# Opening of a fused attention and FFN kernel: the norm weight multiplied earlier, one tile's transposes copied by two engines, and a quarter of a later k load moved forward

## The chip, the cores and the metric

The kernel runs on one core of one Trainium2 chip. The metric is the device time of one execution in microseconds (us), lower is better. Before the change it took 326.73 us (median of 3 runs, 326.69 to 327.09). Engines: PE does matmuls and transposes, PEld loads its weights, DVE is VectorE, ACT is ScalarE, POOL is GpSimd, SP issues most DMAs.

## The reference, cut to what matters

```python
def _attn_ref(q, k, v):                      # q, k, v: (8, 8, 576, 64), float32
    # phi(x) = concat(relu(x) * cos, relu(x) * sin), angle grows with the position
    kv  = einsum('bhsf,bhsd->bhfd', phi(k), v);  z = sum(phi(k), axis=2)
    return einsum('bhsf,bhfd->bhsd', phi(q), kv) / (einsum('bhsf,bhf->bhs', phi(q), z)[..., None] + 1e-6)

def _moe_ref(x, w_gate, w_val, w_out, rms_g):  # x: (4608, 512), d_ff 1536
    xn = x / sqrt(mean(x * x, -1) + 1e-6) * rms_g
    g = xn @ w_gate
    return (g * sigmoid(g) * (xn @ w_val)) @ w_out
```

The argument concerns the first 128 rows of x ("tile 0"). They must pass attention, the norm and a transpose before the first FFN matmul can start. Almost everything before that matmul is a chain of small, dependent steps; everything behind it is dense PE work.

## The kernel before: the parts that matter

```python
    load_kv("k", 0, *LOW); load_kv("k", 0, *HIGH); load_q_tokens(0, 0, 2)
    ...                                       # v of batch 0
    load_q_tokens(0, 2, 4)                    # last load of the opening on SP
...
def x_sq(b, j):        # ACT: sum of squares; POOL: rs = ms ** -0.5 (128x1)
    nc.scalar.activation(out=scr, in_=xt[:, 0 : DM + 1], func=AF.Square, scale=..., accum_out=ms)
    nc.gpsimd.tensor_tensor(out=rs, in0=ms, in1=mhalf, op=ALU.pow)

def x_norm(b, j):      # DVE: xn = (x * rs) * g in one pass, fp32 to bf16
    nc.vector.scalar_tensor_tensor(out=xn, in0=x_of[(b, j)][:, 0:DM], scalar=rs, in1=gb,
                                   op0=ALU.mult, op1=ALU.mult)
...
    kvz_mm(0, high_banks, (2, 3))
    nd_half(0, 0, 0, psV[0]);  nd_post_half(0, 0, 0, psV[0])    # tile 0, heads 0 to 3
    q_tr_evac(A, 0, 1, psO[0][:, :], (0, 4))
    ...
    nd_half(0, 0, 1, psO[1]);  nd_post_half(0, 0, 1, psO[1])    # tile 0, heads 4 to 7
    q_tr_evac(A, 0, 1, psO[0][:, :], (4, 8));  q_phi(A, 0, 2, 1)
    x_sq(0, 0)
    nd_pe(0, 1, psA);  nd_post(0, 1, psA)                       # tile 1
    q_phi(A, 0, 2, 0);  x_sq(0, 1)
    ...
    q_tr_pe(0, 2, psO[0][:, :])               # transposes of q, tile 2
    x_norm(0, 0)
    q_tr_evac(A, 0, 2, psO[0][:, :])          # ACT copies them out of PSUM
    q_phi(A, 0, 3, 1)                         # ACT: half of the q feature map of tile 3
    filler(1, psV[1][:, :])                   # a PE matmul on nothing
    ...
    x_tr_pe(0, 0, psG[1][:, :])               # four 128x128 transposes of xn
    x_tr_evac(V, 0, 0, psG[1][:, :])          # one DVE copy
    x_norm(0, 1);  q_phi(V, 0, 3, 0)
    open_ffn(0, (0, 1), 0, 128)               # the first FFN matmuls
    x_tr_pe(0, 1, psV[1][:, :]);  x_tr_evac(V, 0, 1, psV[1][:, :])
    nd_pe(0, 2, psA);  nd_post(0, 2, psA)     # needs q tile 2
    q_tr_pe(0, 3, psO[1][:, :])               # needs both halves of the map of q tile 3
```

In the timelines below each engine runs its instructions in the order of the program.

## Time and profile before

| | before |
|---|---|
| time, median of 3 | 326.73 us |
| span of the profile | 325.0 us |
| PE busy | 97% of the span |
| share of PE in the chain that ended last | 91% |
| first matmul of k times v | 10.86 us |
| first FFN matmul | 17.66 us |
| first matmul of the third gate slice | 22.35 us |

From the page of before: busy time by engine, and the chain by engine.

```profile
PE 316.5 (97%) x2410; PEld 161.8 (50%) x2445; DVE 185.8 (57%) x412; ACT 176.7 (54%) x366; POOL 31.9 (10%) x67
...
PE 91%; DMA 2%; ACT 2%; DVE 2%; issue 1%; SPq 1%
```

The kernel is bound by PE. So a change to other engines pays only where PE has holes. From the chain of waits of before, 10 to 24 us, in order of time; columns are start, length, who:

```profile
...
14.53 0.72 ACT scr L375 x2
15.25 0.62 ACT qp L209
15.88 0.05 issue
15.92 0.62 PE psO L254 x8
16.54 0.21 PE psV L466
16.76 0.40 PE psG L412 x4
17.16 0.02 issue
17.18 0.43 DVE xnT L265
17.62 0.04 issue
17.66 0.38 PE psG L566 x4
```

L466 is the filler, L412 the transposes of xn and L566 the FFN. From 17.66 us on PE goes gap-free for tens of us (the first wait is one of 0.30 us at 52.4). PE waited for the DVE copy only from 17.16 to 17.66 us, and for xn a little before that (the filler hides it). That is the ground the change wants to win.

The timeline of PE in before; columns are start, length, instruction, count, and in brackets the idle time before it:

```profile
10.86 0.20 PE L282 MATMUL psG<-vvm,kpm 64*128 64x65 bf16 x1
...
17.66 0.38 PE L566 MATMUL psG<-xnT,wg 128*128 128x128 bf16 x4 [0.52 <-DVE xnT L265]
...
18.77 0.41 PE L310 MATMUL psA<-kvzs,qpT 128*128 128x65 bf16 x8
19.02 0.61 PE L254 MATMUL psO<-ident,qp 128*128 128x128 bf16 x8
...
22.35 1.04 PE L566 MATMUL psO<-xnT,wg 128*128 128x256 bf16 x8
```

These lines serve as a ruler. "Third gate slice" stands for the first matmul with the third slice of w_gate (columns 512 to 767), into bank psO. It starts 22.35 - 10.86 = 11.49 us after the first k-times-v matmul, and the first FFN matmul 6.80 us after it. Note also that the transposes of q tile 3 (L254) follow the eight attention matmuls (L310) at 0.25 us, start to start: PE did not wait there.

### The profile page before, as it was taken

Reading aid. Unit: us, or ns where it says so; the run is one execution under the profiler, and the core shown is the slowest. Engines: PE = TensorE matmul, PEld = TensorE weight load, DVE = VectorE, ACT = ScalarE, POOL = GpSimd, SP = SyncE. Lnnn points to the kernel's source line nnn. Section 1 sums busy time; section 2 is a strip of 40 time slices with the busy share of each in tenths; the row PEclk is TensorE's granted clock in tenths of the full one; section 3 lists DMA queues with packets and bytes.
Section 4 is the critical chain, followed back from the end, with each engine's and each line's share of the span. In section 5 each row is a group of like instructions: output and inputs, shape, how many; then the busy total and the mean of one; then the engine's idle time right before and its main releaser. Section 6 shows DMA issues by size and latency. Waiting matters only on the chain.

```text
span 325.0 us, 6411 instructions
## 1 busy us (share of the span) xinstructions
PE 316.5 (97%) x2410; PEld 161.8 (50%) x2445; DVE 185.8 (57%) x412; ACT 176.7 (54%) x366; POOL 31.9 (10%) x67
## 2 busy tenths in 40 slices
PE   8899999999999999999999999999999999999995
PEld 2588465554445444554454445444544444444443
DVE  6875768787766765578257745773577134203410
ACT  6963865965674567545664475556644233223321
POOL 1660112001100110010001100110011000000000
PEclk9999999999999999999999999999999999999999
DMA  7999999998699666976597569957621400020014
GB/s 258 235 189 268 326 185 314 323 185 194 158 257 262 177 163 192 215 195 187 158 217 211 164 188 221 192 157 218 123 43 32 131 32 0 20 111 0 1 34 97
DMA packets 80305, 53.91 MB, mean 166 GB/s; under 512 B 51345, under 2 KB 67729, under 8 KB 80274
## 3 DMA queue, kind: packets, MB, share of 16 engines
q1 hardware_dynamic: 73232, 48.64, 57.7%
q0 software_dynamic: 6880, 4.72, 10.0%
q8 instruction: 19, 0.31, 0.4%
q10 hardware_dynamic: 162, 0.13, 0.2%
q14 instruction: 12, 0.10, 0.1%
HBM read 37.75 MB, written 9.44 MB: 145 GB/s over the span
## 4 chain that ended last, share of the span: by engine, by line
PE 91%; DMA 2%; ACT 2%; DVE 2%; issue 1%; SPq 1%
PE psC L446 26%; PE psG L426 26%; PE psV L426 26%; PE psA L282 3%; DMA rv<-in_v_dram 2%; PE psA L310 2%; PE psG L446 2%; PE psG L566 1%; PE psV L566 1%; PE psO L566 1%; ACT kpm L209 1%; PE psV L254 1%; ACT sg L435 0%; SPq L79 0%; PE psA L317 0%
## 5 line engine op out<-in xcount | busy, mean ns | idle before, releaser
L441 DVE TENSOR_TENSOR hT<-psV,sg 128x512 bf16<-128x512 f32 x102 | 70.3, 689 | 93.9 <-PE psV L426 69.1
L435 ACT ACTIVATE sg<-psG 128x512 f32<-128x512 f32 x102 | 60.6, 594 | 64.9 <-PE psG L426 63.4
L426 PE MATMUL psV<-xnT,wv 128*128 128x512 bf16 (+1 forms) x365 | 92.1, 374 | 0.4
L426 PE MATMUL psG<-xnT,wg 128*128 128x512 bf16 (+1 forms) x352 | 90.9, 374 | 0.7
L446 PE MATMUL psC<-wo,hT 128*128 128x512 bf16 x382 | 88.2, 379 | 0.7
L426 PEld LDWEIGHTS <-wv 128*128 128x128 bf16 x416 | 40.7, 98 | 47.4
L446 PEld LDWEIGHTS <-hT 128*128 128x128 bf16 x420 | 40.3, 98 | 46.6
L426 PEld LDWEIGHTS <-wg 128*128 128x128 bf16 x416 | 38.5, 98 | 41.0 <-DVE xnT L265 0.4
L263 ACT COPY osb<-psC 128x512 f32<-128x512 f32 (+1 forms) x33 | 19.1, 578 | 39.6 <-PE psC L446 38.9
L380 POOL TENSOR_TENSOR rs<-ms,mhalf 128x1 f32<-128x1 f32 x36 | 19.8, 549 | 199.4 <-ACT scr L375 199.4
L387 DVE SCALAR_TENSOR_TENSOR xn<-xt,rs,gb 128x512 bf16<-128x512 f32 x36 | 26.8, 746 | 17.1 <-POOL rs L380 17.1
L375 ACT ACTIVATE scr<-xt 128x513 bf16<-128x513 f32 x36 | 22.9, 635 | 22.8 <-DVE xt L364 22.7
L209 ACT ACTIVATE kpm<-rk,tab 128x256 bf16<-128x256 f32 (+1 forms) x78 | 31.9, 477 | 1.7 <-DMA rk<-in_k_dram 1.7
L364 DVE TENSOR_TENSOR xt<-psA,rec 128x512 f32<-128x512 f32 x35 | 24.2, 691 | 1.2
L211 DVE TENSOR_SCALAR kpm<-rk,tab 128x256 bf16<-128x256 f32 (+1 forms) x84 | 22.2, 330 | 2.2 <-DMA rk<-in_k_dram 2.2
L209 ACT ACTIVATE qp<-rq,tab 128x512 bf16<-128x512 f32 x32 | 22.4, 713 | 0.0
L211 DVE TENSOR_SCALAR qp<-rq,tab 128x512 bf16<-128x512 f32 x32 | 15.2, 488 | 0.0
L310 PEld LDWEIGHTS <-qpT 128*128 128x128 bf16 x248 | 11.6, 98 | 6.7 <-issue 0.3
L310 PE MATMUL psA<-kvzs,qpT 128*128 128x65 bf16 x248 | 12.8, 193 | 0.3
L426 PE MATMUL psG<-xnt_tail,wg 128*128 128x512 bf16 x48 | 12.3, 379 | 0.1
L426 PE MATMUL psV<-xnt_tail,wv 128*128 128x512 bf16 x47 | 12.1, 379 | 0.0
L282 PEld LDWEIGHTS <-kpm 64*128 64x128 bf16 x576 | 9.9, 94 | 3.7 <-issue 2.9
(89 smaller groups left out, 169.1 us busy)
## 6 DMA issues: line engine op xcount, KB each, us to landing
out_dram<-osb SPq DMA_DIRECT2D x32, 256.0 KB, 2.7
rk<-in_k_dram SPq DMA_DIRECT2D x20, 288.0 KB, 4.4
rq<-in_q_dram SPq DMA_DIRECT2D x20, 256.0 KB, 3.1
rv<-in_v_dram SPq DMA_DIRECT2D x17, 288.0 KB, 3.2
rv<-in_v_dram SPq DMA_DIRECT2D x5, 576.0 KB, 7.8
rk<-in_k_dram SPq DMA_DIRECT2D x2, 1152.0 KB, 8.4
rq<-in_q_dram SPq DMA_DIRECT2D x2, 1024.0 KB, 8.7
wo<-in_moe_w_out_dram POOLq DMA_DIRECT2D x4, 384.0 KB, 7.1
```

The costliest lines, as they stand in the source:

```text
L209: nc.scalar.activation(out=out_ap, in_=in_ap, func=AF.Relu, scale=scale)
L211: eng.tensor_scalar(out=out_ap, in0=in_ap, scalar1=scale, scalar2=0.0, op0=ALU.mult, op1=ALU.max)
L282: nc.tensor.matmul(banks[c][:, r * E : (r + 1) * E], lhsT=kp_main[b][lo : lo + 64, j, r, :], rhs=vvm[b % 2][lo : lo + 64, r, j, :], start= ...
L310: nc.tensor.matmul(o[:, g, i, :], lhsT=qpT[(b, 0)][:, h, j * P : (j + 1) * P], rhs=kvz_of(b, h), start=True, stop=True,)
L364: nc.vector.tensor_tensor(out=xt[:, 0:DM].rearrange("p (b h d) -> p b h d", b=2, d=D), in0=o[:, :, :, 0:D], in1=rec[:, :, :].unsqueeze(3). ...
L375: nc.scalar.activation(out=scr[:, :], in_=xt[:, 0 : DM + 1], func=AF.Square, scale=1.0 / math.sqrt(DM), accum_out=ms[:, :],)
L380: nc.gpsimd.tensor_tensor(out=rs[:, :], in0=ms[:, :], in1=mhalf[:, :], op=ALU.pow)
L387: nc.vector.scalar_tensor_tensor(out=xn[:, :], in0=x_of[(b, j)][:, 0:DM], scalar=rs_of[(b, j)][:, :], in1=gb[:, :], op0=ALU.mult, op1=ALU. ...
L426: nc.tensor.matmul(pst[bank][:, cols[0] : cols[1]], lhsT=w[:, t, n * P : (n + 1) * P], rhs=x[:, t, cols[0] : cols[1]], start=(t == 0), sto ...
L435: nc.scalar.activation(out=sg[:, :], in_=psG[bank][:, :], func=AF.Silu)
L441: nc.vector.tensor_tensor(out=hTs[blk][:, n, :], in0=psV[bank][:, :], in1=sg[:, :], op=ALU.mult)
L446: nc.tensor.matmul(bank, lhsT=hTs[blk][:, n, j * P : (j + 1) * P], rhs=wo[:, n, :], start=(n == 0), stop=(n == NNT - 1),)
```

## The change

The intent: take half of the norm's arithmetic off the path behind the mean square (x times g runs while ACT squares), drop the filler, copy the transposes with two engines, and use a hole of the DMA queue for a quarter of the next batch's k. The diff, cut to its core:

```diff
     load_q_tokens(0, 2, 4)
+    load_kv("k", 1, 0, 1)
@@
+    def x_gain(b, j, g):                       # DVE, 128x256: xg = x * gb, half g
+        c = slice(g * DM // 2, (g + 1) * DM // 2)
+        nc.vector.tensor_tensor(out=xg[:, c], in0=x_of[(b, j)][:, c], in1=gb[:, c], op=ALU.mult)
+    def x_scale(b, j):                         # DVE, 128x512: xn = xg * rs
+        nc.vector.tensor_scalar(out=xn[:, :], in0=xg[:, :], scalar1=rs_of[(b, j)][:, :], ...)
@@
     nd_post_half(0, 0, 0, psV[0])
+    x_gain(0, 0, 0)
@@
     nd_post(0, 1, psA)
+    x_gain(0, 0, 1)
@@
-    x_norm(0, 0)
-    q_tr_evac(A, 0, 2, psO[0][:, :])
-    q_phi(A, 0, 3, 1)
-    filler(1, psV[1][:, :])
+    x_scale(0, 0)
@@
-    x_tr_pe(0, 0, psG[1][:, :])
-    x_tr_evac(V, 0, 0, psG[1][:, :])
+    for half, (eng, bank) in enumerate(((A, psG[1]), (V, psV[1]))):
+        part = (2 * half, 2 * half + 2)
+        x_tr_pe(0, 0, bank[:, :], part)
+        x_tr_evac(eng, 0, 0, bank[:, :], part)
+    q_tr_evac(A, 0, 2, psO[0][:, :])
+    q_phi(A, 0, 3, 1)
@@
-    d = load_kv("k", 1)
+    d = load_kv("k", 1, 1, 4)
```

More of the change, by code (lines that the diff above doesn't have):

```diff
@@ L383 @@
     xn_of = {}
+    xg = one.tile([P, DM], FP32, name="xg")
+    def x_gain(b, j, g):
+        c = slice(g * DM // 2, (g + 1) * DM // 2)
+        nc.vector.tensor_tensor(
+            out=xg[:, c], in0=x_of[(b, j)][:, c], in1=gb[:, c], op=ALU.mult
+        )
+    def x_scale(b, j):
+        xn = four.tile([P, DM], BF16, name="xn", tag="xn")
+        nc.vector.tensor_scalar(
+            out=xn[:, :], in0=xg[:, :], scalar1=rs_of[(b, j)][:, :], scalar2=None, op0=ALU.mult
+        )
+        xn_of[(b, j)] = xn
     def x_norm(b, j):
@@ L406, in x_tr_dma, with x_tr_pe @@
         nc.sync.dma_start_transpose(out=x_dst(b, j), in_=xn_of[(b, j)][:, :])
-    def x_tr_pe(b, j, bank):
+    def x_tr_pe(b, j, bank, part=(0, NDT)):
         xn = xn_of[(b, j)]
         dst = bank.bitcast(BF16).rearrange("p (t s) -> p t s", s=P)
-        for t in range(NDT):
+        for t in range(*part):
             nc.tensor.transpose(dst[:, t, :], xn[:, t * P : (t + 1) * P], ident[:, :])
```

## The prediction

> What bounds the kernel now. The page of before gives PE 97% busy over a span of 325.0 us, and the chain that ended last is 91% PE. Reading the PE timeline by issue spacing, PE runs gap-free from the first gated-FFN matmul at 17.66 us to the end, except two small waits (0.30 us at 52.4, 0.25 us at 58.0); other apparent holes are single missing records of 0.22 us. So the change can only win in the opening, before 17.66 us, and only what it saves there less any new PE wait it creates.
>
> The opening in before (timeline, chain of waits). x_sq of tile 0 on ACT 14.53 to 15.26, rs on POOL 15.34 to 15.91, xn on DVE (scalar_tensor_tensor) 15.94 to 16.69, one filler on PE, four transposes 16.75 to 17.15, one DVE copy 17.18 to 17.60, first FFN matmul 17.66. PE idles 0.68 us there by spacing, plus 0.16 us before the transposes. That 0.84 us is the ceiling (0.26% of the time).
>
> What changes, costed.
> 1. xn (0.75 us) becomes tensor_scalar from fp32, as the q feature maps are: 0.48 us. Saves 0.27 us.
> 2. It is preceded by two x*g half multiplies. [...] the trace agrees (691 ns at 512, 0.42 us at 256). So 0.42 us each, 0.34 us of spacing. The first falls in a DVE gap at 13.25 to 13.60 (delay about 0.03 us). The second comes after the tile-1 post, ready at 15.38 us, exactly when rs (15.34) is on POOL. [...]
> 3. Transposes in two banks, copied by ACT (128x256, 0.38 us as kvzs) and DVE: from xn to the first FFN matmul 0.97 us becomes about 0.77 us. First FFN matmul about 17.6 (17.2 without the exclusion).
> 4. ACT copies its half before the q tile 2 evacuation (1.01 us) and q feature map of tile 3 (0.72 us), so these slip by 0.6 to 1.0 us: map finished 18.85 to 19.2 instead of 18.21. PE wants the tile-3 transposes at 18.6 to 19.0: a new PE wait of about 0.2 us.
> 5. 288 KB of k behind q. Windows show the queue running at 380 GB/s before 11.5 us and half empty 11.7 to 12.7, until the weights start; the quarter (0.75 us at that rate, an estimate) mostly fits there. Weights may land 0.1 to 0.5 us later. Slack, landing to first use: wv slice 1 1.2 us, wg slice 3 0.7 us, wv slice 3 0.5 us. Little or no stall. Later k is needed at 33.15 and landed 32.62: no gain on PE.
>
> Sum: between -0.3 us and +0.3 us; I take no change. Predicted 326.7 us, range 326.3 to 327.1 (run-to-run spread is 0.4). Faster by over 2% 0.01, within 2% 0.98, slower 0.01.
>
> What would show it: start of the second half multiply against rs (serial or overlapping); xn end near 16.85; first FFN matmul near 17.6; ACT the releaser of the tile-3 q transposes with a PE gap near 19; no PE weight load released by a wg or wv DMA.
>
> What would make it wrong: no exclusion between DVE and POOL (0.2 to 0.4 us faster); weights delayed by the whole 0.75 us (stalls at 22 to 23.5 us, 0.3 us slower); a slow execution state.

"The exclusion": that the second half multiply on DVE and rs on POOL would run one after the other. That was an assumption; no trace of before shows it. It put 0.34 to 0.42 us in series and made xn ready at about 16.85 us, not at 16.45, and from it follow the 17.6 of step 3 and the 16.85 further down. With it the sum came to between -0.3 and +0.3 us, taken as no change, 326.7 us.

## The result, and the profile after

| | before | after |
|---|---|---|
| time, median of 6 and 6 runs | 326.72 us | 326.74 us |
| all runs | 326.69 to 327.09 | 326.58 to 326.96 |
| span of the profile | 325.0 us | 324.8 us |
| first k-times-v matmul | 10.86 us | 10.70 us |
| first FFN matmul | 17.66 us | 17.16 us |
| third gate slice | 22.35 us | 22.04 us |

The ratio is 0.9998, 95% interval 0.9985 to 1.001: the same. A ratio here is the mean time of one kernel's fast runs over that of the other's of the same rounds, so not quite the ratio of the medians quoted.

The profile does show 0.2 us less span. But 0.16 us of the opening was already there at the first k-times-v matmul, where nothing of the change has run but the issue of the k quarter. It is load jitter: the kernel before, run again, had that matmul at 10.64 us. The ruler removes that. PE in after:

```profile
10.70 0.20 PE L283 MATMUL psG<-vvm,kpm 64*128 64x65 bf16 x1
...
17.16 0.38 PE L581 MATMUL psG<-xnT,wg 128*128 128x128 bf16 x4 [0.35 <-ACT xnT L264]
...
18.27 0.41 PE L311 MATMUL psA<-kvzs,qpT 128*128 128x65 bf16 x8
18.70 0.62 PE L255 MATMUL psO<-ident,qp 128*128 128x128 bf16 x8
...
22.04 1.04 PE L581 MATMUL psO<-xnT,wg 128*128 128x256 bf16 x8
```

From the first k-times-v matmul it is now 6.46 us to the first FFN matmul, 0.34 less than before. To the third gate slice it is 11.34 us, only 0.15 less. The difference was lost at one place: the transposes of q tile 3 follow the attention matmuls at 0.43 us instead of 0.25.

The timeline of DVE in after, across the two half multiplies (L390):

```profile
12.67 0.42 DVE L350 TENSOR_TENSOR xt<-psV,rec 128x256 f32<-128x256 f32 x1
13.20 0.42 DVE L390 TENSOR_TENSOR xg<-xt,gb 128x256 f32<-128x256 f32 x1
13.54 0.15 DVE L346 TENSOR_SCALAR rec<-psO 128x4 f32<-128x4 f32 x1
...
15.31 0.41 DVE L390 TENSOR_TENSOR xg<-xt,gb 128x256 f32<-128x256 f32 x1
15.86 0.49 DVE L396 TENSOR_SCALAR xn<-xg,rs 128x512 bf16<-128x512 f32 x1
```

The one pass that made xn of tile 0 in before, on DVE:

```profile
15.94 0.75 DVE L387 SCALAR_TENSOR_TENSOR xn<-xt,rs,gb 128x512 bf16<-128x512 f32 x1 [0.47 <-POOL rs L380]
```

The timeline of POOL in after, at rs of tile 0:

```profile
15.26 0.57 POOL L381 TENSOR_TENSOR rs<-ms,mhalf 128x1 f32<-128x1 f32 x1 [0.38 <-ACT scr L376]
```

The second half multiply (15.31 to 15.72) lies wholly inside rs (15.26 to 15.83), and neither got longer (rs took 0.57 us in before too). The serialization that I had assumed did not happen.

The timeline of ACT in after:

```profile
16.22 0.19 ACT L376 ACTIVATION_READ_ACCUMULATOR scr<-xt 128x1 f32 x1
16.73 0.37 ACT L264 COPY xnT<-psG 128x256 bf16<-128x256 bf16 x1 [0.33 <-PE psG L428]
17.00 1.02 ACT L264 COPY qpT<-psO 128x1024 bf16<-128x1024 bf16 x1
17.90 0.74 ACT L210 ACTIVATE qp<-rq,tab 128x512 bf16<-128x512 f32 x1
```

The same place on ACT in before:

```profile
16.29 0.19 ACT L375 ACTIVATION_READ_ACCUMULATOR scr<-xt 128x1 f32 x1
16.58 1.01 ACT L263 COPY qpT<-psO 128x1024 bf16<-128x1024 bf16 x1
17.49 0.72 ACT L209 ACTIVATE qp<-rq,tab 128x512 bf16<-128x512 f32 x1
```

The map of q tile 3 (the last line of each) ended at 18.21 in before, long before PE wanted it at 19.02. In after it ends at 18.64, and PE starts on its transposes at 18.70.

### The profile page after: what moved, and what is told of

Same layout as the page of the kernel before. It is cut to its first block, busy times and chain, and to the rows that moved or that the text cites. A ratio compares the mean times of both kernels' runs of the same rounds, so it can differ in the third digit from the quotient of the medians.

```text
span 324.8 us, 6415 instructions
## 1 busy us (share of the span) xinstructions
PE 316.5 (97%) x2409; PEld 161.8 (50%) x2444; DVE 186.0 (57%) x414; ACT 176.8 (54%) x367; POOL 31.9 (10%) x67
## 4 chain that ended last, share of the span: by engine, by line
PE 91%; ACT 4%; DVE 2%; issue 1%; DMA 1%; DVEq 0%; ACTq 0%
PE psC L462 26%; PE psG L442 26%; PE psV L442 26%; PE psA L283 3%; PE psA L311 2%; ACT kpm L210 2%; PE psG L462 2%; PE psG L581 1%; DMA rk<-in_k_dram 1%; PE psV L581 1%; PE psO L581 1%; PE psV L255 1%; ACT qp L210 1%; PE psO L255 1%; ACT sg L451 0%
## 5 line engine op out<-in xcount | busy, mean ns | idle before, releaser
L403 DVE SCALAR_TENSOR_TENSOR xn<-xt,rs,gb 128x512 bf16<-128x512 f32 x35 | 26.1, 745 | 16.6 <-POOL rs L381 16.6
L365 DVE TENSOR_TENSOR xt<-psA,rec 128x512 f32<-128x512 f32 x35 | 24.2, 691 | 1.2
L311 PE MATMUL psA<-kvzs,qpT 128*128 128x65 bf16 x248 | 12.8, 194 | 0.3
```

The lines of the kernel that those rows point to most:

```text
L311: nc.tensor.matmul(o[:, g, i, :], lhsT=qpT[(b, 0)][:, h, j * P : (j + 1) * P], rhs=kvz_of(b, h), start=True, stop=True,)
L365: nc.vector.tensor_tensor(out=xt[:, 0:DM].rearrange("p (b h d) -> p b h d", b=2, d=D), in0=o[:, :, :, 0:D], in1=rec[:, :, :].unsqueeze(3). ...
L403: nc.vector.scalar_tensor_tensor(out=xn[:, :], in0=x_of[(b, j)][:, 0:DM], scalar=rs_of[(b, j)][:, :], in1=gb[:, :], op0=ALU.mult, op1=ALU. ...
```

## The experiments

Timed ratios cannot resolve 0.15 us of 327: each has an interval that is about 0.25% wide (0.38% for one). So the ruler on the traces carries the verdicts, and two replicas show how good the ruler is. Distances are from the first k-times-v matmul, in us.

| run | rs starts | xn ends | first FFN | third gate slice | ratio of times (95%) |
|---|---|---|---|---|---|
| before | 4.48 | 5.83 | 6.80 | 11.49 | |
| after | 4.57 | 5.65 | 6.46 | 11.34 | 0.9998 (0.9985 to 1.001) |
| before_again | 4.47 | 5.82 | 6.79 | 11.49 | 1.0005 (0.9986 to 1.0024) |
| after_again | 4.57 | 5.66 | 6.46 | 11.34 | 1.0005 (0.9993 to 1.0017) |
| k_only | 4.47 | 5.82 | 6.79 | 11.49 | 1.0001 (0.9989 to 1.0013) |
| no_k | 4.57 | 5.65 | 6.46 | 11.34 | 0.9998 (0.9986 to 1.001) |
| scale_only | 4.57 | 5.66 | 6.62 | 11.32 | 1.0 (0.9986 to 1.0013) |
| copies_only | 4.47 | 5.83 | 6.63 | 11.51 | 1.0005 (0.9992 to 1.0018) |
| q_split | 4.57 | 5.66 | 6.46 | 11.15 | 0.9991 (0.9978 to 1.0003) |
| q_split_again | 4.56 | 5.65 | 6.46 | 11.15 | 0.9996 (0.9983 to 1.0008) |
| gain_192 | 4.50 | 5.62 | 6.43 | 11.12 | 0.9991 (0.9977 to 1.0004) |
| gain_late | 4.47 | 5.86 | 6.66 | 11.55 | one run, 327.39 us |
| pool_big | 4.58 | 5.97 | 6.78 | 11.66 | one run, 326.96 us |
| pool_big2 | 6.42 | 7.50 | 8.31 | 13.19 | one run, 328.91 us |

From the third gate slice to the last output DMA that ACT issues it is 299.51 or 299.52 us in every one of these traces. So what is won or lost up to the third gate slice reaches that point undiminished, and nothing happens in between.

### before_again: the noise

No edit.

> The kernel before, unchanged, to size the noise. Ratio 1.000 within 0.0005. In the profile the distance from the first k-times-v matmul to the first FFN matmul should be 6.80 us and to the first matmul of the third gate slice pair (into psO) 11.49 us, both within 0.05 us, while the absolute time of the first k-times-v matmul may move by 0.2 us as the loads land. Open question: the weight queue ran at half rate from 15.3 to 16.5 us in the profile of before and not in that of after. If this is chance, the dip is gone or moved here; if it is a property of the kernel before, it stands here at the same place.

The distances repeat within 0.01 us (6.79 and 11.49). The absolute time of the first k-times-v matmul moved to 10.64 us; over all the traces it lies between 10.64 and 11.23 us. That start-up jitter of 0.6 us is larger than any effect of the change. It is probably also a part of why the timed runs spread by several tenths; the runs without a profile have no trace that could show it. The half-rate stretch of the weight queue stands here as well (see no_k).

### after_again: is the gain real?

No edit of the changed kernel.

> The changed kernel, unchanged. My theory: the opening is really shorter by about 0.15 us (PE distance from first k-times-v matmul to third gate slice 11.34 us against 11.49), made of 0.34 us won up to the first FFN matmul and 0.18 us given back in a PE wait at the q transposes of tile 3; ratio 0.9995, hardly visible. Rival: nothing is won and the 0.31 us of the profile is load jitter: then the distance is 11.49 us again.

The distances are 6.46 and 11.34 again, the same as in after to 0.01 us, so the rival falls: 0.15 us is really won. That is 0.05% of the time. The timed ratio was 1.0005, which with its interval says only that the effect is below what runs can show.

### k_only and no_k: the early quarter of k

```diff
# k_only: the kernel before, plus
+    load_kv("k", 1, 0, 1)
-    d = load_kv("k", 1)
+    d = load_kv("k", 1, 1, 4)
# no_k: the changed kernel, with these three lines taken back
```

> The kernel before with only the quarter of k loaded early. My theory: no effect on PE, ratio 1.000; distances as in before (6.80, 11.49). First gate slice lands about 0.5 us later than in before, no PE weight load waits for it; k of batch 1 complete about 1.5 us earlier, used no earlier. Rival: the quarter delays the weights by its whole 0.75 us and PE waits near 22 to 23.5 us: distance to third slice 11.7 or more. If the weight queue's dip at 15.3 us is gone here but stands in before_again, the early k removes it.

> The changed kernel without the early quarter of k. My theory: same as after: distance 11.34 us, ratio 0.9995. Rival: the early k is needed to keep the gain (weights then land at the times of before, wv slice 3 with 0.5 us of slack less the 0.15 us won): if weights bind, a PE wait appears near 23 us.

Both met my theory: k_only has the distances of before, no_k those of after. In k_only the k of batch 1 was complete at 31.28 us instead of 32.62, and PE gained nothing from it. The quarter of k does nothing to PE, in either direction. Where its cost went can be seen in the landings. The first gate slice lands 4.28 to 4.29 us after its issue in the three traces without the early k (before, before_again, no_k), and 4.78 to 5.06 us with it: it does pay about half a us. By the sixth weight slice (the third of w_val), to which the prediction gives the least slack, this is gone: 11.9 to 12.8 us after the first issue with the early k, 12.5 to 12.8 without. It used DMA time that was otherwise idle, as the windows of before and after show (the columns of interest are the last two, DMA share and GB/s; the share sums the time of all packets, so it can exceed 1). Before:

```profile
11.50:12.50 1.00, 0.94 (x42) 0.74 (x36) 0.79 (x3) 0.97 (x4) 1.00 (x2) 1.00 0.63 130
...
15.50:16.50 1.00, 0.69 (x10) 0.51 (x9) 0.56 (x1) 0.98 (x3) 0.40 (x1) 1.00 1.01 103
```

After:

```profile
11.50:12.50 1.00, 1.00 (x40) 0.87 (x39) 0.75 (x4) 0.91 (x3) 1.00 (x2) 1.00 1.13 314
...
15.50:16.50 1.00, 0.65 (x10) 0.54 (x11) 0.71 (x2) 0.91 (x3) 0.35 (x2) 1.00 1.37 179
```

The hole at 11.5 to 12.5 us is the one that the change fills. The second row is the half-rate stretch that I had asked about. It is slow in the three traces without the early k (103, 109 and 131 GB/s) and was 148 to 185 in the first versions with it, but it came back with the early k in gain_192 (97), gain_late (122) and pool_big2 (137). So the early k does not decide it, and its cause stays open. It never reached PE.

### scale_only: the arithmetic alone

```diff
# the changed kernel, but:
     x_scale(0, 0)
+    q_tr_evac(A, 0, 2, psO[0][:, :])
+    q_phi(A, 0, 3, 1)
-    for half, (eng, bank) in ...               # the two-engine copy
+    x_tr_pe(0, 0, psG[1][:, :])
+    x_tr_evac(V, 0, 0, psG[1][:, :])
-    q_tr_evac(A, 0, 2, psO[0][:, :])
-    q_phi(A, 0, 3, 1)
```

> After, but with one DVE copy of all four transposes and ACT's q tile 2 evacuation and q map of tile 3 ahead of it as in before (filler left out). xn ready about 0.35 us earlier than in before relative to the first k-times-v matmul, PE wait before the first FFN matmul stays about 0.5 to 0.7 us. First FFN matmul at 6.4 to 6.5 us after the first k-times-v matmul; no PE wait at the q transposes of tile 3, since ACT's order is the old one. So my theory expects 0.3 us won and kept: distance to third gate slice about 11.15 us. Rival (the split copy is what wins): distance 11.4 or more.

Half a miss. The order of ACT is the old one and there is indeed no new PE wait: what is won up to the first FFN matmul (0.18 us) is kept to the third gate slice (0.17 us). But 0.18 is not the 0.3 that I had expected. xn ends 5.66 us after the first k-times-v matmul against 5.83. The pass itself got 0.26 us shorter (0.75 to 0.49), but rs starts 0.10 us later. gain_late and gain_192 below look for that 0.10.

### copies_only: the two-engine copy alone

```diff
# the changed kernel, but without xg, x_gain and:
-    x_scale(0, 0)
+    x_norm(0, 0)
```

> After, but with the old one-pass norm (0.75 us) on tile 0. From xn end to the first FFN matmul 0.80 us instead of 0.97; first FFN matmul 6.65 us after the first k-times-v matmul. ACT starts its q work 0.65 us or more later than in before, so the PE wait at the q transposes of tile 3 is 0.2 us or more: distance to third gate slice 11.5 us or longer, nothing won. Rival: the split copy wins alone, distance 11.35.

As expected. The copy by two engines brings the first FFN matmul 0.17 us nearer (6.63), and nothing of it is left at the third gate slice (11.51, against 11.49 in before). The timeline of PE in copies_only:

```profile
18.69 0.41 PE L311 MATMUL psA<-kvzs,qpT 128*128 128x65 bf16 x8
19.12 0.62 PE L255 MATMUL psO<-ident,qp 128*128 128x128 bf16 x8
```

The timeline of ACT in copies_only:

```profile
17.15 0.37 ACT L264 COPY xnT<-psG 128x256 bf16<-128x256 bf16 x1 [0.59 <-PE psG L413]
17.42 1.02 ACT L264 COPY qpT<-psO 128x1024 bf16<-128x1024 bf16 x1
18.33 0.73 ACT L210 ACTIVATE qp<-rq,tab 128x512 bf16<-128x512 f32 x1
```

The spacing at the q transposes is 0.43 us again, and they begin 0.06 us after ACT's map ends. ACT stood idle for 0.59 us before its share of the copy, while the q work that it could have done waited behind it in program order.

### q_split: undo what gives the gain back

```diff
# the changed kernel, with half of the q tile 2 copy moved to DVE, before its share of the transposes
+    q_tr_evac(V, 0, 2, psO[0][:, :], (0, 4))
     for half, (eng, bank) in ...
         ...
-    q_tr_evac(A, 0, 2, psO[0][:, :])
+    q_tr_evac(A, 0, 2, psO[0][:, :], (4, 8))
```

> After, with half of the q tile 2 evacuation moved to DVE, into its idle 0.49 us before it copies the transposes. If ACT's late q map of tile 3 is what costs the 0.18 us PE wait, ACT finishes it about 0.4 us earlier and the wait goes: distance from first k-times-v matmul to third gate slice about 11.16 us, first FFN matmul unchanged at 6.46 to 6.5. Rival: the wait has another cause (bank psO, DVE map of tile 3) and stays.

It met the expectation to 0.01 us: first FFN matmul at 6.46, third gate slice at 11.15. The timeline of ACT in q_split:

```profile
17.16 0.59 ACT L264 COPY qpT<-psO 128x512 bf16<-128x512 bf16 x1
17.64 0.72 ACT L210 ACTIVATE qp<-rq,tab 128x512 bf16<-128x512 f32 x1
```

The timeline of PE in q_split:

```profile
18.39 0.41 PE L311 MATMUL psA<-kvzs,qpT 128*128 128x65 bf16 x8
18.64 0.61 PE L255 MATMUL psO<-ident,qp 128*128 128x128 bf16 x8
```

ACT's copy is 0.59 us instead of 1.02, the map ends at 18.36, ahead of PE, and the spacing is 0.25 us as in before. This shows that the late map on ACT was the cause, and so what had been put in front of it: the whole 0.34 us is now kept. (The map of q tile 3 has a second half, on DVE. DVE has more to do in q_split, and the wait went all the same.)

> The best version so far again, to narrow its time: distance to the third gate slice 11.15 us, 0.34 less than before; ratio to before about 0.999.

The second set of runs has the same distance (11.15). Its ratio is 0.9996 after 0.9991; both intervals include 1. By the traces this version is 0.34 us (0.1%) faster than before; by the clock it is not distinguishable.

### gain_late and gain_192: the 0.10 us of the first half multiply

```diff
# gain_late: the changed kernel, with both halves behind the post of tile 1 (nd_post: attention divided by its sum)
-    x_gain(0, 0, 0)
@@
     nd_post(0, 1, psA)
+    x_gain(0, 0, 0)
     x_gain(0, 0, 1)
# gain_192: q_split, with 192 and 320 columns instead of 256 and 256
-        c = slice(g * DM // 2, (g + 1) * DM // 2)
+        c = slice((0, 192)[g], (192, DM)[g])
```

> After, with both half multiplies behind the post of tile 1, none in the DVE gap. My theory: rs back at 4.48 us after the first k-times-v matmul, but now DVE gates xn: the multiplies start at 4.51 and 4.85 and xn starts at 5.32 instead of 5.16, so first FFN matmul 6.62 and third gate slice 11.5. Rival: rs stays at 4.57, then the gap multiply was not what delayed it.

> The version with the q evacuation split, but x times g cut into 192 and 320 columns instead of 256 and 256. In after and every variant with the half multiply in the DVE gap, rs of tile 0 starts 4.56 to 4.58 us after the first k-times-v matmul, against 4.47 to 4.48 without it, so I think the half multiply overruns the gap by 0.10 us. With 192 columns it should overrun by 0.03 to 0.05: rs at 4.51 to 4.53, xn 0.05 us earlier, first FFN matmul at 6.41, third gate slice at 11.10. Rival (the 0.10 comes from elsewhere, as a longer ACT wait): rs stays at 4.57 and the third slice at 11.15 or later.

gain_late put rs back to 4.47 us, so the first half multiply is what delays it. It paid for that elsewhere: xn started at 5.38 instead of 5.17, because now DVE itself was late (third gate slice 11.55). gain_192 had rs at 4.50 and the third gate slice at 11.12. The direction is as expected, the size a little smaller (11.10 expected): xn now starts 0.07 us after rs has ended, behind the longer second multiply on DVE. The timeline of DVE in gain_192:

```profile
13.04 0.42 DVE L350 TENSOR_TENSOR xt<-psV,rec 128x256 f32<-128x256 f32 x1
13.56 0.36 DVE L390 TENSOR_TENSOR xg<-xt,gb 128x192 f32<-128x192 f32 x1
13.84 0.15 DVE L346 TENSOR_SCALAR rec<-psO 128x4 f32<-128x4 f32 x1
```

The next instruction starts 0.28 us behind a multiply of 192 columns, and 0.34 us behind one of 256 (after: 13.20 and 13.54). The DVE gap that the multiply fills is only as long as PE's next result leaves it (in before DVE stood idle there for 0.34 us, until PE's psO).

Most of the overrun has a cause that I had overlooked. In after the first half multiply starts 0.11 us after the end of the instruction whose result it reads. In the whole trace 77 DVE instructions wait only for the result of the DVE instruction before them, and all of these start 0.03 to 0.04 us after its end. The multiply differs in that it waits for two semaphores, DVE's and one of ACT (ACT made gb, the norm weight, long before), and a separate EVENT_SEMAPHORE instruction stands in front of it on DVE's queue (0.02 us, at 13.13 us; `--source L390` lists it). gain_192 has the same (0.10 us), and there the pass that makes xn, which also has such an instruction in front of it, starts 0.11 us after the multiply instead of 0.03 us after rs. Without the extra 0.07 us the overrun would have been about the 0.03 us that I had predicted. That is arithmetic on the traces: no run took the extra wait away.

### pool_big and pool_big2: do DVE and POOL exclude each other?

```diff
# the changed kernel, with one (pool_big) or two (pool_big2) dummy instructions on POOL ahead of rs
+    nc.gpsimd.tensor_tensor(out=xts[4][:, 0:DM], in0=gb[:, :], in1=gb[:, :], op=ALU.mult)
     x_sq(0, 0)
```

xts[4] is free at that time; the results stay correct.

> After, with a dummy GpSimd multiply of 128x512 fp32, both inputs in SBUF, placed on POOL just before rs of tile 0, so that it runs while DVE does the second half of x times g (two SBUF inputs). The dummy starts at about 14.9 us and lasts an unknown time, I guess over 1 us. If such instructions exclude each other, the half multiply (otherwise at 15.3 us) starts only when the dummy ends, or lasts much longer than 0.41 us. If they don't, it starts at 15.3 us and lasts 0.41 us. In after it lay wholly inside rs (15.26 to 15.83), unhindered, but rs is a 128x1 instruction. rs and everything after it is later here, so this is slower by about the dummy's length less 0.4 us.

POOL was free early in this run, and the dummy (14.28 to 15.38 us) ended just as the half multiply started (15.32 us, 0.42 us long). The run tells little about the dummy. But rs, which followed it, took 0.88 us instead of 0.57, and that is the whole 0.32 us by which this kernel is later than after. The timeline of POOL, then of DVE, in pool_big:

```profile
15.28 0.88 POOL L381 TENSOR_TENSOR rs<-ms,mhalf 128x1 f32<-128x1 f32 x1
...
15.32 0.42 DVE L390 TENSOR_TENSOR xg<-xt,gb 128x256 f32<-128x256 f32 x1
```

The half multiply lies inside rs here too, and this time rs got longer and not the multiply. The dummy in front is not enough to explain it: in pool_big2 rs also follows a dummy, with no half multiply beside it, and took 0.57 us (it starts 0.04 us before that dummy's end, here 0.10 us before it, which accounts for 0.06 us at most). So it looks as if here the multiply held rs, that is, as if the two can exclude each other after all. One run shows it; it is not proven.

> In pool_big the dummy (1.10 us) ended at 15.38 us just as the half multiply started at 15.32, so it told little. Here two dummies in a row, about 2.2 us from 14.3 to 14.9 us on, so that the second half multiply, otherwise 4.61 us after the first k-times-v matmul, falls within one. If two instructions with SBUF inputs exclude each other across DVE and POOL, it starts only after a dummy ends, or lasts 0.7 us or more, or the dummy that meets it lasts longer than 1.10 us by about 0.4. If not, it starts at 4.61 and lasts 0.41 and both dummies last 1.10.

Here the multiply fell in a dummy. The timeline of DVE in pool_big2:

```profile
13.64 0.60 DVE L390 TENSOR_TENSOR xg<-xt,gb 128x256 f32<-128x256 f32 x1
...
15.33 0.69 DVE L365 TENSOR_TENSOR xt<-psA,rec 128x512 f32<-128x512 f32 x1
15.94 0.74 DVE L390 TENSOR_TENSOR xg<-xt,gb 128x256 f32<-128x256 f32 x1
```

The timeline of POOL in pool_big2:

```profile
15.29 1.10 POOL L560 TENSOR_TENSOR xt<-gb 128x512 f32<-128x512 f32 x1
16.46 1.11 POOL L561 TENSOR_TENSOR xt<-gb 128x512 f32<-128x512 f32 x1
```

The second multiply, 0.41 to 0.42 us in all other kernels with 256 columns, took 0.74 us. Its end (16.68) less its usual length is 16.26, near the end of the first dummy at 16.39: it seems to have been held for most of the overlap. The instruction before it (L365), which reads one operand from PSUM, overlapped the same dummy and kept its 0.69 us. For the second multiply that is what an exclusion would look like. But it is one run, and in the same trace the first multiply (13.64 us) took 0.60 us instead of 0.42 although no dummy ran before 15.29 us; what held that one is unknown, and the same cause could have lengthened the second. So an exclusion is possible here, not shown.

## Why the prediction was right, and where its steps failed

The time was right: 326.7 predicted, 326.74 measured, range 326.3 to 327.1. The reason for it was half right, and the time could not tell. As costed, the steps put the third gate slice 0.14 us later than in before (0.06 us won up to the first FFN matmul, then a wait of 0.2 us); by the ruler it came 0.15 us earlier. Both lie inside the stated range (0.4 us to either side) and inside the run-to-run spread. So "no change" was safe because every term was smaller than the spread, and the right number says nothing for the mechanism. The prediction had named "no exclusion between DVE and POOL (0.2 to 0.4 us faster)" as what would make it wrong; that happened, 0.34 us up to the first FFN matmul, and the time still came out right.

- "PE runs gap-free from the first gated-FFN matmul ... So the change can only win in the opening": right. The 299.51 us behind the third gate slice are the same in all traces.
- Step 1, the pass saves 0.27 us: right, 0.75 to 0.49 in after.
- Step 2, "The first falls in a DVE gap ... (delay about 0.03 us)": mis-sized. It was 0.10 us. In after the multiply starts 0.11 us after the end of the instruction whose result it reads (13.09 to 13.20), and it occupies DVE for 0.34 us; I had let it start at once. 0.07 us of that goes with the extra semaphore instruction in front of it. gain_late and gain_192 confirm the place.
- Step 2, the term (0.34 to 0.42 us in series, xn ready at about 16.85): wrong. This is the step that failed, and it rested on the assumption alone. Beside the 128x1 rs the multiply was not held at all: 0.41 us, inside the 0.57 us of rs, and 0.41 us again in after_again and no_k. In before, too, one of the 36 rs (16.56 to 17.11 us) overlaps the last 0.13 us of an xn pass (15.94 to 16.69), and neither is longer than usual (0.55 and 0.75 us). But pool_big, where rs took 0.88 us with the multiply beside it, and pool_big2, where the multiply took 0.74 us beside a dummy of 1.10 us, warn against the rule that the two engines never hold each other; the doubts are named there. xn ended at 16.35 in absolute time; by the ruler it was 0.18 us earlier than in before, instead of 0.16 later.
- Step 3, from xn to the first FFN matmul 0.77 us: 0.81 measured (16.35 to 17.16). copies_only shows 0.17 us for it alone.
- Step 4, a new PE wait of about 0.2 us at the tile-3 transposes: right. It is 0.18 us, present in after, after_again, no_k and copies_only, absent in before, scale_only and q_split. q_split removes it by moving half of one ACT copy to DVE.
- Step 5, the early k with little or no stall: right. k_only and no_k differ from their partners by 0.01 us at most.

The sum that the traces support: 0.17 from the arithmetic (a pass shorter by 0.26, less an rs later by 0.09) and 0.17 from the copy make about 0.34 up to the first FFN matmul; 0.18 is given back; 0.15 is left. The run-to-run spread is larger than that.

## What to carry to other kernels

Moving work onto an engine that looks idle also moves everything behind it in that engine's order (here the map of q tile 3 ended at 18.64 us instead of 18.21, and PE waited 0.18 us): before you split a copy over two engines, ask what the second one would have done in the meantime, and who waits for that. Where an effect is below the noise of the clock, measure from an anchor inside the trace to another one; here that repeated to 0.01 us while whole runs spread by 0.4 us or more. Here PE is gap-free behind the opening, and an earlier load of data that PE does not wait for was worth nothing. And the instruction put into a gap cost more than its own length here: with one more semaphore to wait for than its neighbours, it started 0.11 us after the end of the instruction that it reads, they 0.03 to 0.04.
